# A Fourier filter and a gated MLP on one core: another way to the first layer norms, and another order of the first loads

## The chip, the cores and the metric

The kernel runs on one core of a Trainium2 chip. The core has TensorE (PE in the profile; its weight loads are shown apart as PEld), VectorE (DVE), ScalarE (ACT), GpSimd (POOL) and SyncE (SP), which here only issues DMAs. The time is the device time of one execution in microseconds (us). Lower is better.

## The reference

One input `A_x` of 2048 rows by 512 columns is normalized per row. Two branches work on the normalized rows, and their results are added to the input:

```python
def _layernorm(x, axis=-1, eps=1e-5):
    m = jnp.mean(x, axis=axis, keepdims=True)
    v = jnp.var(x, axis=axis, keepdims=True)
    return (x - m) / jnp.sqrt(v + eps)

xn = _layernorm(A_x, axis=-1)
# A: irfft2(rfft2(xn) * (w_r + 1j * w_i)), over rows and columns
# B: g = xn @ w_gate; u = xn @ w_up; h = gelu(g) * u; h @ w_down   (512 -> 1792 -> 512)
out = A_x + A(xn) + B(xn)
```

All inputs and the output are bfloat16.

## The kernel before

**Tiling.** The 2048 rows are kept as 16 "columns" of 128 rows each (`x_v`: row 16p + c is partition p of column c). The MLP works in four blocks (`sb`) of four columns. For a block, the normalized rows are transposed into `xnT[sb]`, so that the 512 features lie on the partitions in four pieces `e`. The hidden dimension of 1792 is 14 pieces `f` of 128.

**The layer norm** (`layernorm`, L405; `normalize`, L415). For each column VectorE makes statistics (`bn_stats`, L403) and mean and variance (`bn_aggr`, L410), adds eps into `ve` (L411), GpSimd raises `ve` to the power -0.5 into `rstd` (L417), and VectorE writes the normalized `xn` (L423). Columns 0 and 1 are done alone and `xn` in two halves of 256 features; the others in groups of two or four columns.

**The transposes.** Columns 0 and 1 are transposed by TensorE (`pe_transpose`, L427): two 128x128 transposes a half into a PSUM tile `tp`, then a copy to `xnT`, the first half by ScalarE, the second by VectorE (L440). All other columns are transposed by a DMA on SP's queue (`dma_transpose`, L446).

**The MLP products** (`glu`, L493). One call takes `n` columns from `c0` and `nf` pieces of the hidden dimension: a gate product `g_ps` and an up product `u_ps` (both L508), each into one PSUM bank of which there are two; then ScalarE's gelu to `ge` (L525) and VectorE's multiply to `hT` (L533), which frees the banks. For block 0 the calls are: column 0 with pieces 0 to 3, column 1 with pieces 0 to 3, columns 0 and 1 together with pieces 4 to 13 two at a time, then columns 2 and 3 with all pieces two at a time. The first up product of all is 16 matmuls with `Wu`'s first four pieces.

**The loads.** They are issued in the order of the code on SP's queue, with two on ScalarE's: column 0, column 1, half of the first four pieces of `Wg` (`load_first`, L337; the other half on ScalarE's queue), the first four pieces of `Wu` in one transfer (L348), then by `load_w` (L321) pieces 4 to 7 of `Wg`, columns 2 and 3, pieces 4 to 7 of `Wu`, pieces 8 to 11 of both, 12 and 13 of both, and columns 4 to 7. After the transposes of columns 2 and 3 follow columns 8 to 11, the table `RF_t` and columns 12 to 15.

**Warm-up.** Ten matmuls of 128x512 on a constant tile (`dummies`, L389) run before any input is there. ScalarE runs one gelu on a constant (L346), so that its table is loaded early.

**The filter branch.** The Fourier transforms are matmuls with constant tables (L591, L634, L656, L777, L828), with ScalarE evictions between them, VectorE's multiplications with the filter (L677 to L737) and SBUF-to-SBUF moves (L760). They run between the MLP products of blocks 1 to 3. At the end the down product (L882) and the last step of the inverse transform (L886) share a PSUM bank, and VectorE adds the input.

**Order.** All operations are given to a planner (`_Plan`) with an engine, an assumed duration, dependencies, a priority and, for loads, a due time (`land`) at which they are assumed to arrive. It simulates the engines and writes down, engine by engine, the order in which operations start. This order is the program's; each engine then works strictly in it, waiting only for what its instructions need. Another assumed duration or arrival in one place can so change the order in another.

Of the kernel before, what the change touches and what calls it, by code (L numbers as in the profile page):

```python
# [10 lines left out]
P = 128  # L11
# [209 lines left out]
def kernel(  # L221
# [62 lines left out]
    def dve(n, fn, deps, prio, **k):  # L284
        return add("DVE", n, fn, deps, prio, lag=0.08, **k)
# [4 lines left out]
    def pe(n, fn, deps, prio, **k):  # L290
        return add("PE", n, fn, deps, prio, lag=PSUM_LAG, **k)
# [16 lines left out]
    def load(nbytes, fn, deps=(), eng="SP", prio=-1000.0, **k):  # L308
        n_dma[0] += 1
        return dma(nbytes, fn, deps, n_dma[0] + prio, eng=eng, **k)  # L310
# [4 lines left out]
    def load_x(c0, n, land, eng="SP", deps=(), **kw):  # L315
        q = nc.sync if eng == "SP" else nc.scalar
        o = load(2 * n * P * D, lambda: q.dma_start(out=x_t[:, c0:c0 + n], in_=x_v[:, c0:c0 + n]), deps, eng=eng, land=land, **kw)
        for c in range(c0, c0 + n):
            XD[c] = o

    def load_w(f0, f1, lands, mid=lambda: None, deps=(), **kw):  # L321
        a, b = f0 * P, f1 * P
        os = []
        for t, v, land in ((Wg_sb, wg_v, lands[0]), (Wu_sb, wu_v, lands[1])):
            os.append(load(NE * P * P * (f1 - f0), lambda t=t, v=v: nc.sync.dma_start(out=t[:, :, a:b], in_=v[:, :, a:b]), deps, **kw,
                           land=land))
            if len(os) == 1:
                mid()
        for f in range(f0, f1):
            WD[f] = [[o] for o in os]  # L330
# [6 lines left out]
    def load_first(e, eng):  # L337
# [1 line left out]
        return load(P * P * 8, lambda: q.dma_start(out=Wg_sb[:, e:e + 2, 0:4 * P], in_=wg_v[:, e:e + 2, 0:4 * P]), eng=eng,  # L339
                    land=5.1)  # L340

    load_x(0, 1, 3.15)
    d_ident = load_ct("ident", "ident", "ACT", land=2.9)
    load_x(1, 1, 4.2)
    d_g = [load_first(e, eng) for e, eng in ((0, "ACT"), (2, "SP"))]
    add("ACT", 1.3, lambda: nc.scalar.activation(out=eps[:, 1:2], in_=eps[:, 0:1], func=AF.Gelu_apprx_tanh),  # L346
        (o_eps,), -900)
    d_u = load(NE * P * P * 4, lambda: nc.sync.dma_start(out=Wu_sb[:, :, 0:4 * P], in_=wu_v[:, :, 0:4 * P]), land=7.0)  # L348
    for f in range(4):
        WD[f] = [d_g, [d_u]]  # L350
    load_w(4, 8, (8.4, 10.9), lambda: load_x(2, 2, 9.6))
    load_w(8, 12, (12.2, 13.6))
    load_w(12, 14, (14.3, 15.0))
    load_x(4, 4, 17.3)
    g_idx = add("POOL", 0.8, lambda: nc.gpsimd.dma_start(out=idx_t[:], in_=idx_d), (), -10, lag=3.0)
    d_tw = []
    def rows_at(s, g):
# [21 lines left out]
    o_mem = [add("POOL", 0.3, lambda: nc.gpsimd.memset(warm[:], 1.0), (), -20, lag=0.05),  # L379
             add("POOL", 0.2, lambda: nc.gpsimd.memset(half[:], -0.5), (), -15, lag=0.05)]  # L380
    wb = _Buf("S")
    NWARM, NGAP, GAP = 10, 1, 2

    def warm_mm(w):
        if "warm" not in tiles:
# [19 lines left out]
    def layernorm(c0, n, due, after=(), halves=1):  # L405
        k = slice(c0, c0 + n)
        ag = []
        for c in range(c0, c0 + n):
            s = dve(0.6, lambda c=c: stats(c), [XD[c]] + list(after), due - 3.0 + 0.01 * (c - c0))
            ag.append(dve(0.15, lambda c=c: V.bn_aggr(out=mv[:, c], in_=tiles["st", c][:]), (s,), due - 3.2, ))  # L410
        e = dve(0.07, lambda: V.tensor_scalar(  # L411
            out=ve[:, k], in0=mv[:, k, 1], scalar1=EPS, scalar2=None, op0=ALU.add), ag, due - 5)
        normalize(c0, n, due, e, halves)

    def normalize(c0, n, due, e, halves, mean=None, op=ALU.subtract):  # L415
        k = slice(c0, c0 + n)
        r = add("POOL", 0.28 + 0.275 * n, lambda: nc.gpsimd.tensor_tensor(  # L417
            out=rstd[:, k], in0=ve[:, k], in1=half[:, k], op=ALU.pow), (e, o_mem[1]), due - 5, lag=0.1)
        for c in range(c0, c0 + n):
            XN[c] = []  # L420
            for h in range(halves):
                d = slice(h * D // halves, (h + 1) * D // halves)
                XN[c].append(dve(0.06 + 0.29 / halves, lambda c=c, d=d: V.tensor_scalar(  # L423
                    out=xn[:, c, d], in0=x_t[:, c, d], scalar1=mv[:, c, 0:1] if mean is None else mean,
                    scalar2=rstd[:, c:c + 1], op0=op, op1=ALU.mult), (r,), due - 2.5))

    def pe_transpose(c, due):  # L427
        XT[c] = []
        n = len(XN[c])
        for h in range(n):  # L430
            b = _Buf("S")
            es = range(h * NE // n, (h + 1) * NE // n)

            def mm(h=h, es=es):
                psum(f"tp.{c}.{h}", [P, NE, P], BF16)
                for e in es:
                    nc.tensor.transpose(tiles[f"tp.{c}.{h}"][:, e], xn[:, c, e * P:(e + 1) * P], ident)

            def ev(h=h, es=es, eng=(nc.scalar.copy, V.tensor_copy)[h]):
                eng(out=xnT[c // 4][:, es[0]:es[-1] + 1, c % 4], in_=tiles[f"tp.{c}.{h}"][:, es[0]:es[-1] + 1])  # L440

            o = pe(0.24 / n, mm, (XN[c][h], d_ident), due - 2, new=(b,))
            XT[c].append((act, dve)[h](0.1 + 0.35 / n, ev, (o,), due - 30, use=(b,)))

    def dma_transpose(c, due):
        XT[c] = [dma(320e3, lambda: nc.sync.dma_start_transpose(out=xnT[c // 4][:, :, c % 4], in_=xn[:, c]),  # L446
                    XN[c], due - 30, lag=1.0)]

    layernorm(0, 1, -28, (), 2)
    layernorm(1, 1, -25, (), 2)  # L450
    pe_transpose(0, -28)
    dummies(GAP, -29.9, XN[0], P)
    pe_transpose(1, -25)
    for c0, n, due in ((2, 2, -40), (4, 2, 14), (6, 2, 16), (8, 4, 24), (12, 4, 32)):
        layernorm(c0, n, due, XN[max(c0 - 4, 1)])
        for c in range(c0, c0 + n):
            dma_transpose(c, due)
        if c0 == 2:
            load_x(8, 4, 0.0, deps=XN[3], prio=-80.0)
            d_rf = load(P * NC * P * 2, lambda: nc.sync.dma_start(  # L460
                out=RF_t[:], in_=rf_d.rearrange("p (c k) -> p c k", c=NC)), XN[3], prio=-80.0)
            load_x(12, 4, 0.0, deps=XN[3], prio=-80.0)
    d_ct = load_ct("F0", "M0", deps=XN[11], prio=0.0)

    for k in range(2):
# [27 lines left out]
    def glu(c0, n, f0, nf=1, extra=()):  # L493
        sb, o, w = c0 // 4, (c0 % 4) * P, n * P
        gb, ub, eb = _Buf("G"), _Buf("U"), _Buf("ge")
        key = f"{c0}.{n}.{f0}"
        t = now[0]
        dur = NE * (w / 2400.0 + 0.0024)
        now[0] += 2 * dur * nf + 0.2

        def rhs(e):
            return xnT[sb][:, e, c0 % 4:c0 % 4 + n, :].rearrange("p c q -> p (c q)")

        def mm(nm, W, tag, a, b):
            if a == 0:
                psum(f"{nm}.{key}", [P, D], tag=tag)
            for f, e in sorted(((f, e) for f in range(a, b) for e in range(NE)), key=lambda k: (k[1] // 2, k)):
                nc.tensor.matmul(tiles[f"{nm}.{key}"][:, f * w:f * w + w], lhsT=W[:, e, (f0 + f) * P:(f0 + f + 1) * P],  # L508
                                 rhs=rhs(e), start=(f + e == 0), stop=(f == nf - 1 and e == NE - 1),
                                 skip_group_check=nf > 1)  # L510

        g = [o for c in range(c0, c0 + n) for o in XT[c]]
        step = 4 if n == 1 else min(nf, 2)
        us = []
        for a in range(0, nf, step):
            deps = g[-1:] if a else g
            new = [([], []), ([gb], [ub])][a == 0]
            g = [pe(step * dur, lambda a=a: mm("g_ps", Wg_sb, "G", a, a + step), deps + WD[f0 + a][0], t,
                    new=new[0], use=(gb,))]
            us = [pe(step * dur, lambda a=a: mm("u_ps", Wu_sb, "U", a, a + step), us + g + WD[f0 + a][1], t,  # L520
                     new=new[1], use=(ub,))]

        def ge():
            e = work(f"ge.{key}", [P, D], "ge")
            nc.scalar.activation(out=e[:, 0:nf * w], in_=tiles[f"g_ps.{key}"][:, 0:nf * w], func=AF.Gelu_apprx_tanh)  # L525

        a = act(0.1 + nf * w / 1200.0, ge, g, t - 40, new=(eb,), use=(gb,))

        def mul():
            out = hslot(sb, f0)[:, o:o + w]  # L530
            if nf > 1:
                out = tiles["hT", sb][:, f0:f0 + nf, o:o + w]
            V.tensor_tensor(out=out, in0=tiles[f"u_ps.{key}"][:, 0:nf * w].rearrange("p (f w) -> p f w", w=w)  # L533
                            if nf > 1 else tiles[f"u_ps.{key}"][:, 0:w],
                            in1=tiles[f"ge.{key}"][:, 0:nf * w].rearrange("p (f w) -> p f w", w=w)
                            if nf > 1 else tiles[f"ge.{key}"][:, 0:w], op=ALU.mult)

        h = dve(0.08 + nf * w / 960.0, mul, us + [a] + list(extra), t - 40, use=(ub, eb))
        for c in range(c0, c0 + n):
            HT.setdefault(c, []).append(h)  # L540
        return h
# [395 lines left out]
```

## Time and profile before

| | |
|---|---|
| median of 4 runs | 178.98 us (178.5 to 179.32) |
| time of the profiled execution | 179.01 us |
| its span, first to last instruction | 177.2 us |
| PE busy | 172.3 us, 97% of the span |
| DVE busy | 118.9 us, 67% |
| ACT busy | 85.7 us, 48% |
| POOL busy | 17.0 us, 10% |
| DMA | 19.51 MB, mean 110 GB/s |

The span is counted from the first instruction of the program to the last; the time of the execution has 1.8 us around it. A row of the timeline has the start, the duration from the first to the last of its instructions, the engine, the line, the operation, the tiles (out<-in) with their shape, the count, and in brackets the idle time before it with what ended it. "q" behind an engine is its queue or sequencer. A row of the timeline merges neighbours of one kind. A DMA lands later than it is issued; the rows show issues, the landings are seen from who waited for them.

### The profile page before, as it was taken

The page shows a single profiled execution, that of the slowest core. Times are in us where ns is not written, and L with a number is a line of the kernel's source. Part 1 is how long each engine was busy: PE and PEld are TensorE (multiplying, and loading weights), DVE is VectorE, ACT ScalarE, POOL GpSimd, SP SyncE. Part 2 cuts the span into 40 slices and gives each one's busy share as a digit, 9 for nine tenths or more (in the row PEclk, how much of TensorE's full clock was granted, in tenths as well). Part 3 has the DMA queues.
Part 4 walks back from the last instruction along what each step waited for, and adds up shares of the span by engine and source line. Part 5 has one row for each costly group of instructions (what it writes and reads, how often), then busy time and mean ns, then how long its engine had stood idle before and what let it go on. Part 6 is the DMA issues. An engine that isn't in the chain of part 4 may idle for free.

```text
span 177.2 us, 3153 instructions
## 1 busy us (share of the span) xinstructions
PE 172.3 (97%) x1154; PEld 98.2 (55%) x1154; DVE 118.9 (67%) x268; ACT 85.7 (48%) x156; POOL 17.0 (10%) x33
## 2 busy tenths in 40 slices
PE   6899999999999999999999999999999999999993
PEld 2698898654555554445455555454555444444463
DVE  2589799999942657999979998930076732632522
ACT  3224274274578984279989989440243211211100
POOL 3210112008870000000000000000000000000000
DMA  5999944269949900022211222020004242222212
GB/s 142 347 356 259 306 115 91 59 154 237 211 148 325 296 0 0 0 54 60 54 30 46 59 52 53 20 59 4 0 0 153 86 122 89 89 83 65 82 40 59
DMA packets 23215, 19.51 MB, mean 110 GB/s; under 512 B 9568, under 2 KB 21856, under 8 KB 23200
## 3 DMA queue, kind: packets, MB, share of 16 engines
q1 hardware_dynamic: 22464, 17.84, 36.4%
q0 software_dynamic: 320, 1.19, 2.7%
q10 hardware_dynamic: 416, 0.30, 0.6%
q8 instruction: 9, 0.15, 0.3%
q14 instruction: 6, 0.05, 0.1%
HBM read 13.28 MB, written 2.10 MB: 87 GB/s over the span
## 4 chain that ended last, share of the span: by engine, by line
PE 92%; DMA 3%; ACT 2%; SPq 1%; issue 1%; DVE 0%
PE u_ps L508 27%; PE g_ps L508 26%; DMA Wu_sb<-in_B_w_up_dram 3%; PE yp L828 2%; PE bp L591 2%; PE gp L777 2%; PE ep L656 2%; PE dp L634 2%; PE yp__2106 L882 2%; PE yp__2079 L882 2%; PE yp__1990 L882 2%; PE yp__1963 L882 2%; PE yp__1932 L882 2%; PE yp__1902 L882 2%; PE yp__1716 L882 2%; PE yp__2132 L882 2%
## 5 line engine op out<-in xcount | busy, mean ns | idle before, releaser
L508 PE MATMUL u_ps<-xnT,Wu_sb 128*128 128x512 bf16 (+2 forms) x296 | 57.7, 327 | 0.4 <-DMA Wu_sb<-in_B_w_up_dram 0.4
L508 PE MATMUL g_ps<-xnT,Wg_sb 128*128 128x512 bf16 (+2 forms) x296 | 57.7, 327 | 0.3 <-ACT xnT L440 0.2
L525 ACT ACTIVATE ge<-g_ps 128x512 bf16<-128x512 f32 x56 | 33.5, 598 | 34.8 <-PE g_ps L508 30.8
L533 DVE TENSOR_TENSOR hT<-u_ps,ge 128x512 bf16<-128x512 f32 x56 | 38.3, 684 | 14.3 <-PE u_ps L508 12.4
L508 PEld LDWEIGHTS <-Wg_sb 128*128 128x128 bf16 x296 | 27.3, 98 | 19.6 <-issue 0.7
L508 PEld LDWEIGHTS <-Wu_sb 128*128 128x128 bf16 x296 | 27.1, 98 | 18.9 <-DMA Wu_sb<-in_B_w_up_dram 0.7
L882 PEld LDWEIGHTS <-hT 128*128 128x128 bf16 x252 | 23.1, 98 | 22.3
L834 ACT CAST yf<-yp 128x512 bf16<-128x512 f32 x16 | 8.9, 590 | 30.5 <-PE yp L828 30.5
L662 ACT CAST E<-ep 64x512 bf16<-64x512 f32 x32 | 18.5, 580 | 0.4
L850 DVE TENSOR_TENSOR lv<-yf 128x512 bf16<-128x512 bf16 x8 | 3.4, 423 | 16.0 <-ACT yf L834 15.6
L403 DVE BATCH_NORM_STATS2 st<-x_t 128x6 f32<-128x512 bf16 x16 | 10.8, 673 | 4.2 <-DMA x_t<-in_A_x_dram 4.2
L783 ACT CAST Gs<-gp 128x512 bf16<-128x512 f32 x16 | 8.7, 594 | 7.0 <-PE gp L777 7.0
L639 ACT CAST ds<-dp 128x512 bf16<-128x512 f32 x16 | 9.0, 587 | 1.5 <-PE dp L634 1.5
L595 ACT CAST Bs<-bp 128x512 bf16<-128x512 f32 x16 | 8.4, 600 | 1.0 <-PE bp L591 1.0
L417 POOL TENSOR_TENSOR rstd<-ve,half 128x2 f32<-128x2 f32 (+2 forms) x7 | 5.6, 803 | 33.2 <-DVE ve L411 33.2
L423 DVE TENSOR_SCALAR xn<-x_t,mv,rstd 128x512 bf16<-128x512 bf16 (+1 forms) x18 | 6.4, 399 | 0.3 <-POOL rstd L417 0.2
L828 PEld LDWEIGHTS <-Gs 128*128 128x128 bf16 x64 | 4.6, 98 | 2.8
L387 PE MATMUL warm<-warm 128*128 128x512 bf16 (+1 forms) x12 | 4.6, 554 | 1.3 <-POOL half L380 1.3
L634 PEld LDWEIGHTS <-Bs 128*128 128x128 bf16 x64 | 4.5, 98 | 2.4
L777 PEld LDWEIGHTS <-F 128*128 128x128 bf16 x64 | 4.4, 98 | 2.4 <-issue 0.2
L693 DVE TENSOR_TENSOR m<-X,TW 128x1024 bf16<-128x1024 bf16 x8 | 5.5, 693 | 0.2
L828 PE MATMUL yp<-CT,Gs 128*128 128x128 bf16 x64 | 5.5, 219 | 0.0
(103 smaller groups left out, 170.0 us busy)
## 6 DMA issues: line engine op xcount, KB each, us to landing
y<-in_A_x_dram SPq DMA_DIRECT2D x16, 128.0 KB, 3.0
F<-F SPq DMA_DIRECT2D x32, 64.0 KB, 2.0
out_dram<-y SPq DMA_DIRECT2D x15, 128.0 KB, 1.7
Wd_sb<-in_B_w_down_dram SPq DMA_DIRECT2D x1, 1792.0 KB
Wu_sb<-in_B_w_up_dram SPq DMA_DIRECT2D x3, 512.0 KB
x_t<-in_A_x_dram SPq DMA_DIRECT2D x3, 512.0 KB
Wg_sb<-in_B_w_gate_dram SPq DMA_DIRECT2D x2, 512.0 KB
Wg_sb<-in_B_w_gate_dram SPq DMA_DIRECT2D x2, 256.0 KB, 7.0
```

Of the source, the lines that this page charges most:

```text
L403: V.bn_stats(out=st[:], in_=x_t[:, c])
L508: nc.tensor.matmul(tiles[f"{nm}.{key}"][:, f * w:f * w + w], lhsT=W[:, e, (f0 + f) * P:(f0 + f + 1) * P], rhs=rhs(e), start=(f + e == 0), ...
L525: nc.scalar.activation(out=e[:, 0:nf * w], in_=tiles[f"g_ps.{key}"][:, 0:nf * w], func=AF.Gelu_apprx_tanh)
L533: V.tensor_tensor(out=out, in0=tiles[f"u_ps.{key}"][:, 0:nf * w].rearrange("p (f w) -> p f w", w=w) if nf > 1 else tiles[f"u_ps.{key}"][:, ...
L595: nc.scalar.copy(out=o, in_=tiles[f"bp.{cg}.{q}"][:].rearrange("p c (r g a) -> p (c r) g a", r=2, a=4))
L634: nc.tensor.matmul(dp[:, q % 2, q // 2], lhsT=Bs[:, q, G].rearrange("p c r a -> p (c r a)"), rhs=FQ[q], start=(q == 0), stop=(q == 3), ski ...
L639: nc.scalar.copy(out=ds[:].rearrange("p (s k t) -> p s k t", s=2, t=2), in_=tiles[f"dp.{G}"][:].rearrange("p s t k -> p s k t"))
L662: nc.scalar.copy(out=tiles[f"E.{g}"][64 * h:64 * h + 64, r], in_=tiles[f"ep.{g}.{h}"][64 * r:64 * r + 64])
L783: nc.scalar.copy(out=o, in_=tiles[f"gp.{g}.{h}"][:].rearrange("p q (n a) -> p (q n) a", a=4))
L828: nc.tensor.matmul(yp[:, q], lhsT=tiles["G"][:, q, c], rhs=IQ[q], start=(q == 0), stop=(q == 3), skip_group_check=True)
L834: nc.scalar.copy(out=tiles[f"yf.{c // 2}"][:, c % 2], in_=tiles[f"yp.{c}"][:])
L882: nc.tensor.matmul(y[:, s], lhsT=tiles[sb, f][:, cl * P:(cl + 1) * P], rhs=Wd_sb[:, f, s], start=(f == 0), stop=False)
```

## The change

It has these parts:

- **Root and reciprocal for columns 0 and 1.** A new `layernorm_sqrt` makes statistics, mean and variance as before, then ScalarE's square root of the variance plus eps into `rstd`, VectorE's reciprocal of it in place, and `xn` in halves. The statistics of column 1 stand behind `xn` of column 0. The early ScalarE activation is now a root; the gelu on a constant comes behind column 1's root.
- **The first up product in halves.** It becomes two groups of eight matmuls (features `e` 0 and 1, then 2 and 3). Column 1's first two transposes stand before the first group and its last two between the groups. Both copies of column 1 to `xnT` are VectorE's.
- **Loads.** The first four pieces of `Wu` come in two transfers. Column 1 is issued behind the half of `Wg` on SP's queue. Columns 4 to 7 are issued ahead of pieces 12 and 13 of the weights. `RF_t` is issued ahead of columns 8 to 15, which come in one transfer.
- **Warm-up.** Eight matmuls in place of ten.

The planner's order changes in other places as a consequence: in VectorE's list the folds and statistics of block 0 stand differently between the multiplies, and in the part with the filter branch of the second half of the MLP the small matmuls and the moves of two neighbouring groups are arranged differently. What the instructions compute is otherwise the same.

```diff
-    load_x(0, 1, 3.15)
+    load_x(0, 1, 3.2)
     d_ident = load_ct("ident", "ident", "ACT", land=2.9)
-    load_x(1, 1, 4.2)
     d_g = [load_first(e, eng) for e, eng in ((0, "ACT"), (2, "SP"))]
-    add("ACT", 1.3, lambda: nc.scalar.activation(out=eps[:, 1:2], in_=eps[:, 0:1], func=AF.Gelu_apprx_tanh),
-        (o_eps,), -900)
-    d_u = load(NE * P * P * 4, lambda: nc.sync.dma_start(out=Wu_sb[:, :, 0:4 * P], in_=wu_v[:, :, 0:4 * P]), land=7.0)
+    load_x(1, 1, 4.8)
+    add("ACT", 1.5, lambda: nc.scalar.activation(out=eps[:, 1:2], in_=eps[:, 0:1], func=AF.Sqrt), (o_eps,), -900)
+    d_u = [load(P * P * 16, lambda e=e: nc.sync.dma_start(out=Wu_sb[:, e:e + 2, 0:4 * P], in_=wu_v[:, e:e + 2, 0:4 * P]),
+                land=(7.1, 7.4)[e // 2]) for e in (0, 2)]
     for f in range(4):
-        WD[f] = [d_g, [d_u]]
+        WD[f] = [d_g, d_u]
     load_w(4, 8, (8.4, 10.9), lambda: load_x(2, 2, 9.6))
     load_w(8, 12, (12.2, 13.6))
-    load_w(12, 14, (14.3, 15.0))
-    load_x(4, 4, 17.3)
+    load_x(4, 4, 16.5)
+    load_w(12, 14, (16.6, 17.0))
...
-    NWARM, NGAP, GAP = 10, 1, 2
+    NWARM, NGAP, GAP = 8, 1, 2
...
+    def layernorm_sqrt(c, due, prev=()):
+        s = dve(0.65, lambda: stats(c), [XD[c]] + list(prev), due - 3.0)
+        a = dve(0.18, lambda: V.bn_aggr(out=mv[:, c], in_=tiles["st", c][:]), (s,), due - 3.2)
+        r = SD[c] = act(0.25, lambda: nc.scalar.activation(
+            out=rstd[:, c:c + 1], in_=mv[:, c, 1:2], func=AF.Sqrt, bias=eps[:, 0:1], scale=1.0), (a, o_eps), due - 60)
+        r = dve(0.12, lambda: V.reciprocal(out=rstd[:, c:c + 1], in_=rstd[:, c:c + 1]), (r,), due - 3.0)
+        XN[c] = []
+        for h in range(2):
+            d = slice(h * 256, h * 256 + 256)
+            XN[c].append(dve(0.24, lambda d=d: V.tensor_scalar(
+                out=xn[:, c, d], in0=x_t[:, c, d], scalar1=mv[:, c, 0:1], scalar2=rstd[:, c:c + 1],
+                op0=ALU.subtract, op1=ALU.mult), (r,), due - 2.5))
...
-            def ev(h=h, es=es, eng=(nc.scalar.copy, V.tensor_copy)[h]):
+            def ev(h=h, es=es, eng=(nc.scalar.copy, V.tensor_copy)[h or k]):
...
             o = pe(0.24 / n, mm, (XN[c][h], d_ident), due - 2, new=(b,))
-            XT[c].append((act, dve)[h](0.1 + 0.35 / n, ev, (o,), due - 30, use=(b,)))
+            TP[c].append(o)
+            XT[c].append((act, dve)[h or k](0.1 + 0.35 / n, ev, (o,), due - 30, use=(b,)))
...
-    layernorm(0, 1, -28, (), 2)
-    layernorm(1, 1, -25, (), 2)
+    layernorm_sqrt(0, -28)
+    layernorm_sqrt(1, -25, XN[0])
     pe_transpose(0, -28)
     dummies(GAP, -29.9, XN[0], P)
-    pe_transpose(1, -25)
+    act(1.5, lambda: nc.scalar.activation(out=eps[:, 1:2], in_=eps[:, 0:1], func=AF.Gelu_apprx_tanh), [SD[1]] + XT[0], -70)
+    pe_transpose(1, -25, 1)
...
-            load_x(8, 4, 0.0, deps=XN[3], prio=-80.0)
             d_rf = load(P * NC * P * 2, lambda: nc.sync.dma_start(
                 out=RF_t[:], in_=rf_d.rearrange("p (c k) -> p c k", c=NC)), XN[3], prio=-80.0)
-            load_x(12, 4, 0.0, deps=XN[3], prio=-80.0)
+            load_x(8, 8, 0.0, deps=XN[3], prio=-80.0)
...
-            us = [pe(step * dur, lambda a=a: mm("u_ps", Wu_sb, "U", a, a + step), us + g + WD[f0 + a][1], t,
-                     new=new[1], use=(ub,))]
+            if c0 + f0:
+                us = [pe(step * dur, lambda a=a: mm("u_ps", Wu_sb, "U", a, a + step), us + g + WD[f0 + a][1], t,
+                         new=new[1], use=(ub,))]
+                continue
+            for k in range(2):
+                us = [pe(step * dur / 2, lambda k=k: mm("u_ps", Wu_sb, "U", 0, step, range(2 * k, 2 * k + 2)),
+                         us + g + TP[1][k:k + 1] + WD[0][1][k:k + 1], t, new=(ub,) if k == 0 else (), use=(ub,))]
+                if k == 0:
+                    TP[1][1].deps += us
```

## The prediction

> **What bounds the kernel now.** Four views, in this order. First the page: the shares of the engines, and the chain that ended last.
>
> ```profile
> PE 172.3 (97%) x1154; PEld 98.2 (55%) x1154; DVE 118.9 (67%) x268; ACT 85.7 (48%) x156; POOL 17.0 (10%) x33
> ...
> PE 92%; DMA 3%; ACT 2%; SPq 1%; issue 1%; DVE 0%
> ```
>
> TensorE is the bound nearly everywhere, so the time is its work plus its gaps. A faster layer norm at the front is worth something only as far as it makes TensorE's later work start sooner. So, second, the timeline of the first microseconds.
>
> ```profile
> 1.34 4.34 PE L387 MATMUL warm<-warm 128*128 128x512 bf16 x10 [1.34 <-POOL half L380]
> ...
> 3.13 0.69 DVE L403 BATCH_NORM_STATS2 st<-x_t 128x6 f32<-128x512 bf16 x1 [3.13 <-DMA x_t<-in_A_x_dram]
> 4.07 0.15 DVE L411 TENSOR_SCALAR ve<-mv 128x1 f32<-128x1 f32 x1
> 4.38 0.58 POOL L417 TENSOR_TENSOR rstd<-ve,half 128x1 f32<-128x1 f32 x1 [2.33 <-DVE ve L411]
> 5.00 0.60 DVE L423 TENSOR_SCALAR xn<-x_t,mv,rstd 128x256 bf16<-128x256 bf16 x2
> 6.25 1.05 PE L508 MATMUL g_ps<-xnT,Wg_sb 128*128 128x128 bf16 x16 [0.20 <-ACT xnT L440]
> 7.14 0.39 PE L437 MATMUL tp<-CT,xn 128*128 128x128 bf16 x4
> 7.89 1.07 PE L508 MATMUL u_ps<-xnT,Wu_sb 128*128 128x128 bf16 x16 [0.36 <-DMA Wu_sb<-in_B_w_up_dram]
> 8.80 1.06 PE L508 MATMUL g_ps<-xnT,Wg_sb 128*128 128x128 bf16 x16
> ```
>
> The first gate product waits for the layer norm, the first up product for its weights (landed 7.85). From 8.80 matmul follows matmul. Third, where that run breaks:
>
> ```profile
> 13.17 3.43 SPq L446 DMA_TRANSPOSE xnT<-xn  x2
> 18.52 1.04 PE L508 MATMUL u_ps<-xnT,Wu_sb 128*128 128x256 bf16 x8
> 18.63 0.69 DVE L403 BATCH_NORM_STATS2 st<-x_t 128x6 f32<-128x512 bf16 x1 [0.84 <-DMA x_t<-in_A_x_dram]
> 19.66 0.78 PEld L508 LDWEIGHTS <-Wg_sb 128*128 128x128 bf16 x8 [0.38 <-issue]
> 19.69 1.03 PE L508 MATMUL g_ps<-xnT,Wg_sb 128*128 128x256 bf16 x8
> ```
>
> The up product of 18.52 is 8 matmuls 0.109 us apart, so a successor could start at 19.39; the next gate product starts at 19.69, after 0.30 us idle. It is the first that reads columns 2 and 3, and the second of their DMA transposes lands at 19.55 in the trace. They queue on SP behind columns 4 to 7, which land at 18.6 (the DVE row). Fourth, the only other break until the end:
>
> ```profile
> 83.71 0.87 PE L777 MATMUL gp<-CT,F 128*128 128x128 bf16 x8
> ```
>
> Eight such matmuls take 0.61 elsewhere; here 0.26 is a wait in their middle, for a ScalarE eviction. From 19.69 to the end the span is thus fixed work plus 0.26.
>
> **The base.** The profiled execution took 179.01 us, its span 177.2 and 1.8 around it; the median of the four runs shown is 178.98, so I take 0.03 off at the end.
>
> **Front, column 0.** Removed: ve (0.15) and POOL's pow (0.58) with two hand-overs; from 4.04, where the aggregate ends, to xn at 5.00 is 0.96. Added: a root on ScalarE and a reciprocal on VectorE, neither in the trace. Nearest rows: the 128x1 ACTIVATE of L346, 0.20, and the 128x1 ve, 0.15; hand-overs 0.16 (DVE to POOL) and 0.04 (POOL to DVE). 0.16+0.20+0.04+0.15+0.04 = 0.59, so xn starts at 4.63, 0.37 sooner. Bounds: 0.4 if hand-overs cost 0.04 each, 0.96 if root or reciprocal costs as much as pow; at worst nothing gained. The warm-up matmuls (0.427 apart) now end near 4.75 instead of 5.52, so they aren't in the way. Transposes 5.1, ScalarE's copy (0.37) 5.5 to 5.87, first half of the gate product near 5.92 instead of 6.25.
>
> **Front, column 1: the added wait.** Its load now stands behind half of Wg on SP's queue. In the trace it is issued at 1.19 and lands 2.5 later, at 3.68; that half of Wg lands at 5.88 (issue 1.65, 4.2 to landing). Column 1 can't beat 4.15 (its issue slips 0.46) and, as the same 800 KB have then gone through, shouldn't be later than 5.88; I take 5.5, nearer the end whose byte count it shares. VectorE's order then runs: statistics 5.53 to 6.21, the copy of column 0's second half (0.29) behind them to 6.53, aggregate to 6.71, root to 7.07, reciprocal to 7.26, xn's first half to 7.64. The second half of the gate product waits for that copy: 6.56 to 7.0. TensorE's order puts column 1's first transposes ahead of the first up half, so everything behind waits for xn: transposes 7.75, up half 7.86 to 8.31 (half of Wu landed by 7.85), transposes to 8.42, up half to 8.87, gate product of column 1 at 8.87 instead of 8.80. So the front gives +0.07; with column 1 landing at 4.8 it would be -0.3 (then Wu's second half, 7.85, binds), at 5.88 +0.45.
>
> **ScalarE.** The gelu table load moves from 1.69 (hidden under the input's landing) to behind the second root: 7.07 to 8.35 (1.28), then the dummy gelu (0.20), so the first ge runs 8.56 to 9.16 instead of 7.34 to 7.94. The gate product that reuses its PSUM buffer starts at 10.58: 1.4 us of cover, cost nothing; without it, up to 0.6. The up product's end plus 0.16 sets hT at the same 9.1 anyway. The Trainium skill (ScalarE: Activation LUTs, What ACT_TABLE_LOAD costs) speaks against the move: 1.28 of load plus 1.38 of drain per switch. The trace shows the load from 1.69 for 1.28 and the ACTIVATE at 2.98, 0.01 after it, so no drain there; by the page the first ge would end at 10.5, still before 10.58, and the sum is the same.
>
> **SP and the weights.** Wu in two pieces adds one issue (0.48). SP has it to spare: its issues end at 11.67 and the transposes wait for xn until 13.17. Columns 4 to 7 now go ahead of the last weights (columns 12 and 13 of the hidden dimension). Before, these landed at 16.5 and 17.2 (issues 6.81 and 8.62, 9.7 and 8.6 to landing) and columns 4 to 7 at 18.6. The bytes are the same, so the last piece of Wu inherits 18.6 and that of Wg about 17.9 (0.73 earlier, as now). They are wanted at 17.64 and 18.52, +0.07. Gate product 17.92, up product 18.79, next gate product at 19.67 at the earliest; the transposes have the same bytes ahead and still land at 19.55, so it starts at 19.69, as before. **A gain at the front ends here**: neither the last Wu nor the transposes come sooner. Cost 0.0; bounds -0.3 (both land 0.3 sooner) to +0.3 (front at +0.45 and transposes 0.2 late).
>
> **Columns 8 to 15 in one piece.** They now land together behind the RF table, when the second half did: 24.1 in the trace, where the first half had landed at 21.6. VectorE's order has column 8's statistics ahead of an hT multiply and those of 9 and 10 ahead of the next. From 24.17, by rows: statistics 0.69, hT 0.68, two xn 0.65, two more statistics with aggregates 1.45, and that next hT ends near 28.3; the up product that needs its PSUM buffer starts at 28.44. Cover 0.1; today that hT ends at 27.45. I take 0.0, as the cover is there; bounds 0 and +0.5.
>
> **Filters (76 to 118 us).** The planner's order there changes though the code does not: up to twelve gp matmuls and four ep stand in a row, and F moves of two groups interleave. Fixed work; what can change is the 0.26 wait. Bounds -0.26 to +0.5 (two such waits more). I take +0.1, as longer runs of matmuls ask more evictions (0.59 each) at once. Two pows off POOL cost nothing: POOL is on no chain here.
>
> Sum: 179.01 + 0.0 (front and stream) + 0.0 (columns 8 to 15) + 0.1 (filters) - 0.03 = **179.1**.
>
> **The clock.** Warm-up matmuls are 0.427 apart, later ones 0.216 for the same 512 columns: TensorE starts at half speed, and the tenth, started at 5.16, gave way after 0.36, so the change came near 5.45. Now eight end at 4.75 and little follows until 5.9. The Trainium skill (TensorE: Matmul & The Clock Gate, Part 1) wants some 3.4 us of sustained activity, in a window that runs free of the kernel; eight times 0.427 is 3.4, just that. By the page alone a window could be missed, and the sum would be as in the second rival.
>
> **Rivals.** *Faster*: column 1 lands by 4.8, the last Wu and the transposes 0.3 sooner, and the wait at 84 goes: 179.01-0.30-0.26-0.03 = 178.42. For it: 0.30 is idle today. Against: the bytes ahead of both are unchanged. 0.17. *Slower by the clock*: half speed past 8 us, for which speaks that eight warm-ups end before the change was seen, against it that the matmuls go on after a short gap. Sixteen 128-column matmuls then take 1.71 instead of 0.89; the gate half and the up product that lie on the path lose about 0.9, the front stands at +1.0, arrival at 20.4 instead of 19.69: 179.7. It decides from a front of +0.85 on, since 0.30 is absorbed. 0.13. *Slower by VectorE*: columns 8 to 15 land at 24.9 instead of 24.1; the hT above ends at 29.1, the up product of 28.44 slips 0.6, and with the filters' 0.1 the time is 179.01+0.7-0.03 = 179.7. For it: VectorE works in order, and one late load holds up the multiplies behind it. Against: the bytes ahead are the same. It decides from a landing of 24.8 on, where the loss passes 0.54. 0.17. That the change does nothing to the end is the forecast itself, 0.53.
>
> A measurement here tells 0.3%, 0.54 us, from nothing. Forecast 179.1, of its own 178.6 to 179.5; range 178.2 to 180.0, from past the faster case to past the slower two, by 0.3 for what the bounds leave open. Faster 0.17, same 0.53, slower 0.30.
>
> **What would show it.** Right: xn near 4.6; column 1's statistics idle before on its load until about 5.5; up half near 7.9; the gate product of columns 2 and 3 still near 19.7 with idle before it. Wrong: that product at 19.3 or sooner (the stream came sooner), warm-like 0.107 spacing after 6 us (clock), an up product near 28.4 waiting for hT.

## The result, and the profile after

The changed kernel takes 179.34 us (median of 52 executions, 178.89 to 180.94), the kernel before beside it 178.94 us (median of 78, 178.38 to 180.82). The ratio is 1.002, with a 95% interval of 1.0011 to 1.003: a loss of 0.2 to 0.5 us that can be told from nothing by its interval, but is smaller than the 0.3% that the prediction had set as its bound. Five executions of each kernel lie above 180 us; they don't move the medians.

The profiled execution took 179.33 us, its span is 177.5 us. The page of the changed kernel, its shares of the engines and the chain that ended last:

```profile
PE 171.7 (97%) x1152; PEld 97.9 (55%) x1152; DVE 119.5 (67%) x269; ACT 87.7 (49%) x159; POOL 15.9 (9%) x31
...
PE 88%; DVE 4%; ACT 3%; DMA 2%; issue 1%; SPq 0%; DVEq 0%
```

TensorE has two warm-ups less to do (172.3 to 171.7 us) and yet the span is 0.3 longer, so there is more idle time. VectorE (0 to 4%) and ScalarE (2 to 3%) have gained shares of the chain; the DMA has lost one (3 to 2%). Taken piece by piece, that chain now runs at the front through column 1's load (issued at 1.66, 4.44 us), its statistics (0.69), its root (0.30) and its `xn` (0.36), where before it ran through the load of `Wu` (issued at 2.12, 5.72 us). The rest of VectorE's share, and of ScalarE's, lies almost all at the filters, from 76 to 95 us. The timeline of the front, rows that answer to those shown of before:

```profile
1.34 3.35 PE L387 MATMUL warm<-warm 128*128 128x512 bf16 x8 [1.34 <-POOL half L380]
...
3.34 0.69 DVE L403 BATCH_NORM_STATS2 st<-x_t 128x6 f32<-128x512 bf16 x1 [3.34 <-DMA x_t<-in_A_x_dram]
...
4.29 0.29 ACT L420 ACTIVATE rstd<-mv,eps 128x1 f32<-128x1 f32 x1 [1.07 <-DVE mv L419]
4.61 0.16 DVE L422 RECIPROCAL rstd<-rstd 128x1 f32<-128x1 f32 x1 [0.36 <-ACT rstd L420]
4.81 0.60 DVE L426 TENSOR_SCALAR xn<-x_t,mv,rstd 128x256 bf16<-128x256 bf16 x2
...
5.96 0.61 PE L526 MATMUL g_ps<-xnT,Wg_sb 128*128 128x128 bf16 x8
...
6.12 0.69 DVE L403 BATCH_NORM_STATS2 st<-x_t 128x6 f32<-128x512 bf16 x1 [0.70 <-DMA x_t<-in_A_x_dram]
6.73 0.27 DVE L457 COPY xnT<-tp 128x256 bf16<-128x256 bf16 x1
...
7.06 0.61 PE L526 MATMUL g_ps<-xnT,Wg_sb 128*128 128x128 bf16 x8 [0.49 <-DVE xnT L457]
7.13 0.29 ACT L420 ACTIVATE rstd<-mv,eps 128x1 f32<-128x1 f32 x1 [1.22 <-DVE mv L419]
...
8.06 0.29 PE L454 MATMUL tp<-CT,xn 128*128 128x128 bf16 x2 [0.40 <-DVE xn L426]
...
9.19 1.06 PE L526 MATMUL g_ps<-xnT,Wg_sb 128*128 128x128 bf16 x16
```

Column 0 gained what was promised: from the start of its statistics to `xn` it is now 1.47 us (3.34 to 4.81), before 1.87 (3.13 to 5.00). Column 1 took it away: its load lands at 6.10, its statistics wait 0.70 for it and stand, on VectorE, ahead of the copy that the second half of the first gate product needs (7.06). Its own `xn` comes at 7.66. The gate product of column 1 starts at 9.19 instead of 8.80.

The timeline where the run used to break, at the first product of columns 2 and 3:

```profile
18.83 1.04 PE L526 MATMUL u_ps<-xnT,Wu_sb 128*128 128x256 bf16 x8
...
19.60 0.86 PEld L526 LDWEIGHTS <-Wg_sb 128*128 128x128 bf16 x8
19.71 1.04 PE L526 MATMUL g_ps<-xnT,Wg_sb 128*128 128x256 bf16 x8
```

The gate product starts at 19.71, 0.02 later than before, but for another reason: no wait stands before it. The second transpose landed at 19.15 (a landing has no row of its own), and TensorE itself came late. So up to here 0.37 of 0.39 us of loss (10.97 against 10.58 at the first product of two columns) have been swallowed by waits that were there anyway: the 0.30 here, and 0.07 at 11.52, where the kernel before waited for pieces 4 to 7 of `Wu`. The rest is made at the filters, in the timeline of the changed kernel around 83 and 94 us:

```profile
80.91 0.39 PE L659 MATMUL dp<-CT,Bs 128*128 128x128 bf16 x4
...
81.40 1.17 ACT L687 CAST E<-ep 64x512 bf16<-64x512 f32 x2
...
81.99 1.03 PE L526 MATMUL u_ps<-xnT,Wu_sb 128*128 128x512 bf16 x4
...
82.59 0.58 ACT L664 CAST ds<-dp 128x512 bf16<-128x512 f32 x1
...
83.23 0.38 PE L681 MATMUL ep<-ds,CT 128*128 128x512 bf16 x1 [0.21 <-ACT ds L664]
...
92.92 1.17 ACT L687 CAST E<-ep 64x512 bf16<-64x512 f32 x2
...
93.65 1.03 PE L526 MATMUL u_ps<-xnT,Wu_sb 128*128 128x512 bf16 x4
94.11 0.58 ACT L664 CAST ds<-dp 128x512 bf16<-128x512 f32 x1
94.75 0.38 PE L681 MATMUL ep<-ds,CT 128*128 128x512 bf16 x1
```

Four up matmuls start 0.216 us apart from 81.99 on, so the next could start at 82.86; `ep` needs the copy `ds`, which ends at 83.17, and so `ep` starts at 83.23, 0.37 late (a row counts the idle time only from the modelled end of the last matmul, hence its 0.21). At 94.75 it is 0.24 late in the same way. The copy itself is late because of its place in ScalarE's list: the last `dp` matmuls before it end at 81.30, but ScalarE first does two evictions `E`, and both times `ds` starts 0.02 us after they end (82.57 and 94.09). Before, there was one wait here, 0.264 us among the `gp` of 83.71, and it is gone. 0.371 + 0.241 - 0.264 = 0.35 us, nearly the whole of the measured loss of 0.40.

### The profile page after: what moved, and what is told of

It reads as the page before. It is cut to its first block, busy times and chain, and to the rows that moved or that the text cites. A ratio compares the mean times of both kernels' runs of the same rounds, so it can differ in the third digit from the quotient of the medians.

```text
span 177.5 us, 3148 instructions
## 1 busy us (share of the span) xinstructions
PE 171.7 (97%) x1152; PEld 97.9 (55%) x1152; DVE 119.5 (67%) x269; ACT 87.7 (49%) x159; POOL 15.9 (9%) x31
## 4 chain that ended last, share of the span: by engine, by line
PE 88%; DVE 4%; ACT 3%; DMA 2%; issue 1%; SPq 0%; DVEq 0%
PE u_ps L526 25%; PE g_ps L526 24%; DMA x_t<-in_A_x_dram 2%; PE yp L853 2%; PE bp L616 2%; PE gp L802 2%; PE ep L681 2%; PE yp__2105 L907 2%; PE yp__2078 L907 2%; PE yp__1989 L907 2%; PE yp__1962 L907 2%; PE yp__1931 L907 2%; PE yp__1904 L907 2%; PE yp__1810 L907 2%; PE yp__1764 L907 2%; PE yp__1725 L907 2%
## 5 line engine op out<-in xcount | busy, mean ns | idle before, releaser
L432 POOL TENSOR_TENSOR rstd<-ve,half 128x2 f32<-128x2 f32 (+1 forms) x5 | 4.9, 976 | 33.7 <-DVE ve L411 33.7
L718 DVE TENSOR_TENSOR m<-X,TW 128x1024 bf16<-128x1024 bf16 x8 | 5.5, 691 | 0.2
L724 DVE TENSOR_TENSOR m<-X,TW 128x1024 bf16<-128x1024 bf16 x8 | 5.5, 684 | 0.0
L659 PE MATMUL dp<-CT,Bs 128*128 128x128 bf16 x64 | 5.4, 219 | 0.0
L681 PE MATMUL ep<-ds,CT 128*128 128x512 bf16 x16 | 5.1, 379 | 0.3 <-ACT ds L664 0.2
```

The source lines that it names most:

```text
L659: nc.tensor.matmul(dp[:, q % 2, q // 2], lhsT=Bs[:, q, G].rearrange("p c r a -> p (c r a)"), rhs=FQ[q], start=(q == 0), stop=(q == 3), ski ...
L681: nc.tensor.matmul(ep[:], lhsT=cc("L" if g + h else "L0"), rhs=tiles[f"ds.{2 * g + h}"][:], start=True, stop=True)
```

## The experiments

The theory was that the new order of the filters' steps is the loss, and that what the front loses is swallowed in the wait for the transposes. Rival A: the late load of column 1 is the loss. Rival B: the eight warm-ups and the clock. Rival C: the reordered loads move nothing, and the transposes' landing of 19.15 us is chance.

**The order of the filters alone.** The planner's order there follows from when its simulation has `tables_fix`, a step of GpSimd, end: 68.03 us before the change, 67.06 after it. One assumed duration puts either order into either kernel. Into the kernel before, and, in the second, into the changed one:

```
-    d_fix = add("POOL", 3.0, tables_fix, d_tw, 60, lag=0.2)
+    d_fix = add("POOL", 1.73, tables_fix, d_tw, 60, lag=0.2)
```
```
-    d_fix = add("POOL", 3.0, tables_fix, d_tw, 60, lag=0.2)
+    d_fix = add("POOL", 4.25, tables_fix, d_tw, 60, lag=0.2)
```

> The kernel before, with one number of its planner changed: the time that the planner assumes for tables_fix (d_fix) goes from 3.0 to 1.73 us. Nothing that is computed, loaded or transposed changes, and the order up to 60 us stays; from 60 to 125 us the filters' steps come in the order that the changed kernel has. Theory (the new order of the filters' steps is the loss): the one wait of 0.264 us at 83.88 goes and two waits of about 0.37 and 0.24 us on ScalarE's ds copies come, so 0.612 - 0.264 = 0.35 us longer than before, 179.3 us, ratio 1.0020. Rival A (the loss is the later load of column 1): no difference, 178.95 us, ratio 1.000. Rival B (the eight warm-ups and the clock): no difference either. Halfway, 1.001, parts them.

> The changed kernel, with the time that the planner assumes for tables_fix (d_fix) at 4.25 us instead of 3.0, which puts the filters' steps back into the order of the kernel before; all that comes before 60 us stays as changed. Theory: the waits of 0.371 and 0.241 us go, one of about 0.26 us comes back, so 0.35 us shorter than the changed kernel: 179.0 us, 1.000 of the kernel before; the front's 0.39 us at the first two-column gate product is still there and is lost in the wait for the transposes of columns 2 and 3. Rival A (the later load of column 1 is the loss): stays at 179.34 us, 1.002 of before. Rival B (warm-ups and clock): stays at 179.34 us as well.

The first took 179.35 us against 178.84 for the kernel before (ratio 1.0027, 1.0009 to 1.0045). Its timeline has the changed kernel's two waits, though its front is the old one:

```profile
83.11 0.38 PE L656 MATMUL ep<-ds,CT 128*128 128x512 bf16 x1 [0.21 <-ACT ds L639]
...
94.63 0.38 PE L656 MATMUL ep<-ds,CT 128*128 128x512 bf16 x1
```

The second took 179.22 us (1.0022, 1.0005 to 1.0039), where 179.0 was expected, and its profiled execution took 180.57: something else was in it (further down). Both were run once more, on another chip, side by side:

> The kernel before with the filters' steps in the order of the changed kernel (tables_fix assumed at 1.73 us), once more beside the run above, to size the two parts on one chip. Theory: +0.35 us by its waits (0.371 + 0.241 - 0.264), 179.2 us, ratio 1.002, none over 180 us. Rival: no difference to before, ratio 1.000.

> The changed kernel with the filters in the order of the kernel before (tables_fix assumed at 4.25 us), once more, since its first profile had half pace from 7.68 to 11.05 us. Theory now: the front of the changed kernel has no slack: what column 1's load is late shows at the end one for one. With that load landing at 5.9 to 6.4 us, as the profiles had it, the gate product of columns 2 and 3 starts at 19.5 to 20.0 us instead of 19.69: 178.8 to 179.2 us, ratio 0.999 to 1.002, and one or two executions of twelve over 180 us from the half pace. Rival (the order of the filters has no part in it): 179.4 us, as the changed kernel itself, ratio 1.003.

The old kernel with the new order took 179.10 us against 178.87 (1.0014, 0.9994 to 1.0035), the changed kernel with the old order 179.20 (1.0026, 0.9997 to 1.0055). In the latter's timeline the `gp` wait of before is back, and no `ep` waits:

```profile
84.04 0.87 PE L802 MATMUL gp<-CT,F 128*128 128x128 bf16 x8
```

So rival A is wrong as the whole cause: the filters' order costs the old kernel 0.2 to 0.5 us by the two medians, with nothing else changed (the second, of six executions, has 1 in its interval). But the filters' order is not the whole cause either: the changed kernel with the old order is still 0.3 to 0.4 us above the kernel before by medians, with intervals that begin near nothing.

**Column 1's load.** The changed kernel with that load first on SP's queue again, and the same with the old filter order:

```
-    d_g = [load_first(e, eng) for e, eng in ((0, "ACT"), (2, "SP"))]
-    load_x(1, 1, 4.8)
+    load_x(1, 1, 4.2)
+    d_g = [load_first(e, eng) for e, eng in ((0, "ACT"), (2, "SP"))]
```

> The changed kernel with column 1's load issued on SP ahead of the half of Wg again (as before the change), everything else as changed, the filters' order too. Theory: column 1 lands near 3.7 us, xn of column 1 no longer ends the front; the first up product of two columns is then held by Wu's second piece at 11.4 us, and the gate product of columns 2 and 3 starts with the transposes at about 19.15 + 0.14 = 19.3 us instead of 19.71, since the transposes' landing of 19.15 us (19.55 before) comes from moving columns 4 to 7 ahead of the last weights: 0.4 us shorter than the changed kernel, 178.95 us, ratio to before 1.000, with the filters' waits of 0.37 and 0.24 us still there. Rival A (the later load is the whole loss): 178.95 us too, but the filters' waits are gone or cost nothing. Rival C (the transposes' earlier landing is chance and not the order of the loads): the product of columns 2 and 3 starts at 19.7 us again and the time stays 179.34 us, ratio 1.002.

> The changed kernel with both edits: column 1's load ahead of Wg's half, and tables_fix assumed at 4.25 us so that the filters come in the order of the kernel before. Theory: the two gains add, 0.40 + 0.35 us: 178.6 us, ratio to before 0.998. Rival A (the later load is the whole loss, the order of the filters is worth nothing): 178.95 us, ratio 1.000. Rival C (the transposes' landing doesn't follow the loads' order): only the filters' 0.35 us are gained, 179.0 us, ratio 1.000.

179.16 us (1.0026, 1.0008 to 1.0043) and 178.73 us (0.9997, 0.9982 to 1.0012). The difference of the two medians, 0.43 us, is about that of the filters' order again. The second of the two against the changed kernel with the old filter order, on the same chip and with the load's place (and assumed landing) as the only edit, is 178.73 against 179.22 us; seven of its twelve executions lie at 178.46 to 178.74, below the lowest of the other, 179.01. So the late load of column 1 is what the front loses, and rival A is right in part. The expected 178.6 was nearly reached, but the front did what was expected only in part: the first product of two columns started at 10.30 us instead of 10.97, and then waited for pieces 4 to 7 of `Wu`, which landed at 11.76 in that execution. Timeline of the first of the two:

```profile
10.30 1.04 PE L526 MATMUL g_ps<-xnT,Wg_sb 128*128 128x256 bf16 x8
11.81 1.05 PE L526 MATMUL u_ps<-xnT,Wu_sb 128*128 128x256 bf16 x8 [0.47 <-DVE ve L411]
```

The wait is put down to VectorE's `ve`, which was not what it needed; the load landed 0.05 ahead of the start. From there on matmul followed matmul, and the product of columns 2 and 3 started at 19.68, not at the 19.3 expected, although the second transpose had landed at 19.09.

**The warm-ups.** The changed kernel unaltered, with `NWARM` at 10 instead of 8, and, with ten, column 1 first and the old filter order (there with 4.1 us for `tables_fix`):

> The changed kernel once more, unaltered, so that it stands on the same chip as the three that follow. Both theories: 179.3 us, ratio to before 1.002. The theory that the clock takes part (matmuls of 128 columns 0.107 us apart instead of 0.056 for some 3.4 us after the start, as two profiles showed, from 7.68 to 11.05 us in one and up to 10.25 us in the other) expects one or two executions of twelve over 180 us; the theory of the filters' order alone expects none.

> The changed kernel with ten warm-up matmuls instead of eight; loads, filters and the rest as changed. Theory (order of the filters +0.35, the front's +0.4 lost in the former wait for the transposes): no change of the median, 179.3 us, since the first gate product's second half waits for VectorE's copy at 7.06 us whatever the warm-ups do. Rival B (eight warm-ups are the loss): 178.95 us, the time of before. For the executions of over 180 us the clock's theory expects fewer, but not none, since the hole from 6.35 to 8.06 us, the load of column 1, stays.

> The changed kernel with column 1's load first, the filters in the order of the kernel before, and ten warm-ups. With eight warm-ups this fell into two groups, seven executions of twelve at 178.5 to 178.7 us and five at 179.3 to 180.0, whose profile (180.0) had the matmuls at half pace up to 10.25 us. Theory with the clock: one group, near 178.6 us, ratio 0.998 to 0.999; the profile at full pace by 6 us. If the warm-ups have no part in it (rival): two groups again in about the same shares, median 178.7 to 179.3 us.

The kernel before took 178.87 us here. 179.41 us (1.003, 1.0017 to 1.0043); 179.51 us with ten warm-ups (1.0034, 1.002 to 1.0047); 178.66 us for the third (0.9991, 0.9974 to 1.0008). Ten warm-ups give nothing back, so rival B is wrong for the median. None of the nine executions of either of the first two was over 180 us, so these runs don't tell whether two more warm-ups make those rarer. In the third, eight of twelve were at 178.29 to 178.79 and four at 179.12 to 179.70: two groups, as with eight warm-ups, where the expectation from the clock had one. The profile, one of the upper four, was at full pace by 6 us. What it waited for was pieces 4 to 7 of `Wu` again, landed at 11.92:

```profile
10.49 1.04 PE L526 MATMUL g_ps<-xnT,Wg_sb 128*128 128x256 bf16 x8
11.96 0.72 PE L526 MATMUL u_ps<-xnT,Wu_sb 128*128 128x256 bf16 x5 [0.44 <-DVE st L403]
```

**The loads alone.** The kernel before with columns 4 to 7 ahead of the last weights (the planner keeps the old landing times, so that nothing else moves); then `RF_t` ahead of columns 8 to 15 as well and these in one piece; then the same in two pieces:

```
-    load_w(12, 14, (14.3, 15.0))
     load_x(4, 4, 17.3)
+    load_w(12, 14, (14.3, 15.0))
```
```
-            load_x(8, 4, 0.0, deps=XN[3], prio=-80.0)
             d_rf = load(P * NC * P * 2, lambda: nc.sync.dma_start(
...
-            load_x(12, 4, 0.0, deps=XN[3], prio=-80.0)
+            load_x(8, 8, 0.0, deps=XN[3], prio=-80.0)
```

> The kernel before with one edit: columns 4 to 7 are loaded ahead of the last two pieces of Wg and Wu, as the change has them (and the planner is given the old landing times, so that no other order changes). Theory: SP's first-in-first-out queue frees the transposes of columns 2 and 3 sooner, their last landing goes from 19.55 to about 19.15 us, the gate product of columns 2 and 3 starts at 19.4 instead of 19.69: 0.3 us gained, 178.6 us, ratio 0.998. Rival C (the landing of the transposes does not follow this order): nothing gained, 178.9 us, ratio 1.000; the product starts at 19.7 us with its wait before it.

> The kernel before with the change's order of loads on SP from columns 4 to 7 on, and nothing else of it: columns 4 to 7 ahead of the last two pieces of Wg and Wu, RF_t ahead of columns 8 to 15, and these in one piece. With the first of the three alone, the gate product of columns 2 and 3 started 0.5 us sooner, but the first product of the filters then waited 0.230 us at 22.59 for RF_t, which landed at 22.88. Theory: with RF_t ahead it lands near 20.4 us, as in the changed kernel, that wait goes, and the gain of 0.3 us at the transposes stays: 178.55 us, ratio 0.998. Rival (the load reorder is worth nothing, or columns 8 to 15 in one piece cost what it gains): 178.87 us, ratio 1.000; then a wait for columns 8 to 15, or for a transpose, stands between 20 and 35 us.

> The run above, with columns 8 to 11 and 12 to 15 as two loads again, both behind RF_t. Theory: the one piece costs nothing, so no difference to the run above, 178.55 us. Rival (VectorE waits for the one long load and holds up the product of 28.4 us): 0.1 to 0.5 us shorter than the run above.

178.88 us (1.0001, 0.9987 to 1.0014), 178.89 us (0.9995, 0.9977 to 1.0013) and 178.90 us (1.0, 0.9978 to 1.0021): nothing, three times. The expectations had 178.55 to 178.6, and they had taken one landing for a rule. Over all profiles the second transpose of columns 2 and 3 landed at 19.55, 19.46 and 19.22 us with the old order of loads, and at 19.01 to 19.93 with the new. Rival C holds: the order makes no difference that stands out from the difference between executions. The first of the three had the early landing (19.07) in its profile and showed what would be late next, `RF_t`, landed at 22.88:

```profile
22.93 0.77 PE L591 MATMUL bp<-RF_t,xf 128*128 128x128 bf16 x11
22.93 0.65 PEld L591 LDWEIGHTS <-xf 128*128 128x128 bf16 x11 [0.24 <-issue]
```

0.23 us were lost there, and with `RF_t` ahead (second and third run) no product waited for it. One piece or two for columns 8 to 15 made no difference.

**All profiles in one table.** Start of the first gate product of columns 2 and 3, and from there to the start of the last matmul of the kernel:

| kernel | front | product of columns 2, 3 | from there to the last | filters' order |
|---|---|---|---|---|
| before | old | 19.69 | 154.58 | old |
| before, new filter order | old | 19.59 | 154.92 | new |
| the same again | old | 19.35 | 154.92 | new |
| before, columns 4 to 7 first | old | 19.20 | 154.81 | old (and 0.23 for `RF_t`) |
| before, new loads | old | 19.61 | 154.59 | old |
| the same in two pieces | old | 19.64 | 154.58 | old |
| after | new | 19.71 | 154.92 | new |
| after, again | new | 19.54 | 154.94 | new |
| after, ten warm-ups | new | 19.98 | 154.93 | new |
| after, old filter order, again | new | 20.01 | 154.58 | old |
| after, old filter order | new | 21.27 (half pace) | 154.59 | old |
| after, column 1 first | new | 19.68 | 154.94 | new |
| the same, old filter order | new | 20.70 (half pace) | 154.59 | old |
| the same, ten warm-ups | new | 19.84 | 154.58 | old |

From about 20 us on, the time is the order and nothing else: 154.58 to 154.59 or 154.92 to 154.94 in all profiles but the one that waited for `RF_t`, and from the last matmul's start to the end of the execution it is 4.7 us in all. The filters' order is thereby shown and sized: 0.34 to 0.35 us. What differs from execution to execution lies before 20 us, and hangs on where loads land and, in the two profiles marked, on the clock.

The front can be read from the same profiles. From the first product of two columns to that of columns 2 and 3 TensorE takes 8.73 to 8.74 us if nothing makes it wait. In the three profiles of the old front with the old loads that first product starts at 10.45 to 10.58, and TensorE is then idle for 0.17 to 0.30 us before the product of columns 2 and 3, which starts 0.13 to 0.14 after the second transpose has landed: there is slack. With the changed front there is none: column 1's load landed at 5.93, 6.10 and 6.41 us, and the product of columns 2 and 3 started at 19.54, 19.71 and 20.01, each time 13.60 or 13.61 later (13.55 in the profile with ten warm-ups). VectorE's statistics of column 1 and that product, in the timeline of the run at 20.01:

```profile
6.43 0.69 DVE L403 BATCH_NORM_STATS2 st<-x_t 128x6 f32<-128x512 bf16 x1 [1.21 <-DMA x_t<-in_A_x_dram]
```
```profile
20.01 1.04 PE L526 MATMUL g_ps<-xnT,Wg_sb 128*128 128x256 bf16 x8
```

The mean of these three is 19.75; that of the three profiles of the old front with the old loads (19.69, 19.59, 19.35) is 19.54. That makes the front about 0.2 us of loss, from few executions. The two medians agree with such a size, no better: the whole loss was 0.40 and 0.54 us, and 0.35 of it are the filters. Against the kernel before, the size of the front's part stays open between nearly nothing and 0.4 us; against the changed kernel with column 1 first it is 0.5 us by the medians above.

## Why the prediction was right, and where it wasn't

The forecast was 179.1, within 0.3% of before with a chance of 0.53, in a range of 178.2 to 180.0. The result is 179.34 against 178.94: inside the range, and within the bound, on the side of the loss. The sum is 0.24 short, and its filters step alone is 0.25 short; that the larger miss at the front, 0.39 against 0.07, hardly shows in the time is a matter of the waits that happened to stand behind it. By its steps:

- **Front, column 0** held. 0.40 us gained from statistics to `xn`, 0.37 predicted; root 0.29 (0.20 assumed), reciprocal 0.16 (0.15), and the hand-over to ScalarE 0.04 (0.16 assumed), so two misses cancel. `xn` came at 4.81 and not 4.63 because the load itself landed 0.2 later in this execution. As foreseen, it is worth nothing by itself.
- **Front, column 1** had the right mechanism, the copy behind the statistics and the transposes behind `xn`, and the wrong size. The load landed at 6.10 us, taken at 5.5 and bounded by 5.88: the bound was wrong, since it took one execution's landing of another piece as the latest. The loss at the first product of two columns is 0.39, where +0.07 was taken and +0.45 the upper end.
- **"A gain at the front ends here"** was right, and so is its mirror: most of the loss ended there too (19.71 against 19.69). That the transposes' landing does not follow from the order of the loads held in so far as no order moved it beyond the spread between executions, though in the profile of the changed kernel itself it came 0.4 sooner than said (19.15). "From 8.80 matmul follows matmul" overlooked the 0.07 us at 11.52. The last pieces of `Wg` and `Wu` landed at 17.34 and 18.12, about 0.5 sooner than said, and no product waited for them. What the step didn't have is that TensorE's idle 0.3 us differs between executions (0.17 to 0.30 in three), and that the front loses 0.4: then nothing is left of it, and a still later load of column 1 passes through one for one.
- **Filters** is the step that was mis-sized: +0.1 was taken, +0.35 measured, inside its bounds of -0.26 to +0.5. The one wait went and two others came: `ep` now comes up before ScalarE, busy with two `E`, has made its `ds` copy. The evictions were named, but the number of waits was guessed. No run moved that copy alone.
- **ScalarE** held: the table load behind the second root took 1.28 us and the first gelu ran 8.84 to 9.42, wanted at 10.97. The Trainium skill (ScalarE: Activation LUTs, What ACT_TABLE_LOAD costs) adds a drain of 1.38 us to such a switch; here, in mid-kernel, the ACTIVATE started 0.01 us after the load, so no drain is seen:

```profile
7.13 0.29 ACT L420 ACTIVATE rstd<-mv,eps 128x1 f32<-128x1 f32 x1 [1.22 <-DVE mv L419]
7.44 1.28 ACT L471 ACT_TABLE_LOAD   x1
8.73 0.20 ACT L471 ACTIVATE eps<-eps 128x1 f32<-128x1 f32 x1
```

- **Columns 8 to 15 in one piece** cost nothing, as taken: no product waited for them, and two pieces made no difference. They landed at 22.89, sooner than the 24.1 forecast, and at 22.89 to 24.48 over all profiles with this load, so the rival "slower by VectorE" never met its condition of 24.8.
- **The clock**: as a cause of the median refuted, by the pace in the profile and by the run with ten warm-ups. As a mechanism it is real, in single executions: see the last section. The rival had priced it at an arrival of 20.4 us and 179.7; one profile in which the full pace came at 10.3 us (of the kernel with column 1 first and the old filter order) arrived at 20.70.
- **Faster** asked for column 1 by 4.8 us, which never happened with its load in that place.

## What to carry to other kernels

Where a planner writes the order, an edit at the front may cost most at a place that it does not touch: find the number that the order hangs on, put the new order into the old kernel by that number alone, and the part is sized to some 0.02 us by the distance between two matmuls, long before a median of many executions can tell. Before a landing time is used as a bound, see how it differs between executions: here the same load landed 0.5 us apart, and a reordering "worth" 0.4 us by one profile was worth nothing in three runs. A wait that swallows a loss is slack only in the executions in which it is there.

No version here is shown to beat the kernel before: the nearest is the changed kernel with column 1 first, ten warm-ups and the old filter order, 178.66 us, ratio 0.9991 with 1 in its interval.

## What was not expected of the hardware

Half pace of TensorE (matmuls twice as far apart) well into the products came in two forms, both seen in kernels with eight warm-ups. In the first profile of the changed kernel with the old filter order TensorE was at full pace by 5.0 us, then stood idle for 1.2 us from 6.13 on (column 1 landed at 6.40), and from 7.68 to 11.05 us matmuls of 128 columns stood 0.107 us apart instead of 0.056. The view by stretches shows it in the column of the granted clock (the third from the right):

```profile
6.00:7.00 1.00, 0.35 (x7) 0.23 (x5) 0.58 (x1) 0.00 (x0) 0.00 (x0) 1.00 1.02 355
7.00:8.00 1.00, 0.64 (x8) 0.52 (x7) 0.60 (x5) 0.55 (x2) 0.00 (x0) 0.82 1.10 390
8.00:9.00 1.00, 0.79 (x9) 0.65 (x8) 0.77 (x3) 1.00 (x1) 0.00 (x0) 0.50 1.07 371
9.00:10.00 1.00, 1.00 (x12) 1.00 (x11) 0.23 (x2) 0.71 (x3) 0.00 (x0) 0.50 1.09 360
10.00:11.00 1.00, 1.00 (x13) 1.00 (x10) 0.36 (x2) 0.00 (x0) 0.00 (x0) 0.50 1.10 349
11.00:12.00 1.00, 1.00 (x20) 1.00 (x19) 1.00 (x2) 0.15 (x1) 0.00 (x0) 0.97 1.09 345
```

The stretch is 3.37 us long, and the execution took 180.57 us; its granted clock has a mean of 0.989 over the whole. That mean is on record for every execution of the changed kernel and of the experiments: it is 0.989 or 0.990 in four, of 180.57, 180.61, 180.72 and 180.94 us, all with eight warm-ups and the late load of column 1, and 0.998 or more in all others. So half pace for such a stretch very likely stands behind these four, though only the first was profiled. That the hole before it is the reason is not shown; the other profiles of that front have holes there of 0.65 to 0.74 us and no half pace after them. In the profile with column 1 first and the old filter order the pace was half until 10.3 us, and the granted clock stands at 1.00 all the same; only the rows tell, sixteen matmuls in 1.87 us instead of 1.06:

```profile
7.00:8.00 1.00, 1.00 (x12) 1.00 (x11) 0.63 (x3) 1.00 (x1) 0.00 (x0) 1.00 1.12 377
```
```profile
6.28 1.87 PE L526 MATMUL g_ps<-xnT,Wg_sb 128*128 128x128 bf16 x16
```

Its execution took 180.01 us. So the pace has to be read from the distance of matmuls of one shape, not from the granted clock alone. The Trainium skill (TensorE: Matmul & The Clock Gate, Part 1) says that the gate decides by a window of some 3.4 us that runs free of the kernel, so that the turn to full pace varies, by 0.5 us either way. The length of 3.37 us agrees, and so does it that the turn varies: in two profiles of the changed kernel, unaltered, the last transpose of column 0 (5.54 and 5.29 us) stands 0.056 us from the next matmul in one and 0.107 in the other. The spread is wider than the page has it: turns were seen at about 4.6, 5.0, 5.5, 6.3 and 10.3 us. What share of the other executions above 180 us half pace explains, and whether two warm-ups more change that share, is open: before had five of 78 with ten warm-ups, after five of 52 with eight; of the experiments' executions up to two of twelve (and one of six) were above 180 us with eight, up to one of twelve with ten.
